# Attention over channels and a mixture of experts on one Trainium2 core: loads moved to GpSimd's queue, and the last block ended tile by tile over four pieces

## The chip, the core and the metric

The kernel runs on one core of one Trainium2 chip. The metric is the time of one execution in device microseconds (us). The core has five engines with an instruction queue each: TensorE (PE in the profile, its weight loads PEld), VectorE (DVE), ScalarE (ACT), GpSimd (POOL) and SyncE (SP). Each works through its own queue in order, and waits there for semaphores that others raise. SP does no arithmetic: it issues DMA transfers. GpSimd issues some too.

## The reference: what is computed

Channel attention over B = 4 batches of N = 5056 tokens with C = 256 channels, whose result goes into a mixture of eight experts, where each token goes to one expert alone:

```python
qn = q / (norm(q, axis=1) + 1e-06); kn = k / (norm(k, axis=1) + 1e-06)
a = softmax(kn.transpose(0, 2, 1) @ qn / tau, -1)         # per batch, 256 x 256
x = (v @ a).reshape(20224, 256)
logits = x @ w_gate + modality_bias[modality_id]          # 20224 x 8
e_idx = argmax(logits, 1); gate_w = softmax(logits, -1)[rows, e_idx]
out[mask] = gate_w[mask, None] * (relu(x[mask] @ w1[e]) @ w2[e])   # mask: e_idx == e, F = 1024
```

Norms run over the tokens of a batch, for each channel. All tensors are float32; `modality_id` is an int64 of 0 or 1.

## The kernel before

**Stages.** Batch 0's gram matrix (k transposed times q) is formed in ten steps of 512 tokens (the last is shorter). Then come its norms, its softmax and the product with v. From there on 40 token groups of 512 follow each other; group g is (batch, step) = divmod(g, 10). Each group is multiplied with its batch's attention matrix, its gates are computed, every token is given a place in its expert's part of a row buffer `xs` in DRAM, and its row is scattered there. From group 2 on, a block of 512 such rows of one expert is taken per group, so that 40 blocks (slots 0 to 39; the last two have three tiles of 128 rows, the others four) run through the expert's two matrix products, and the rows are scattered to `out`. The later batches' gram steps are laid between these. Blocks past slot 39 exist as conditional code, which this input does not reach.

**The gram, `kq_pieces`.** SP fetches q and k of a step (L305), TensorE multiplies (L355; in the order's rows `g`), ScalarE squares (L344, into `sq`), VectorE adds the squares into `acc` (L346). After step 9 VectorE folds `acc` (L402), TensorE sums over partitions (L405 and L407, `ns`), ScalarE and VectorE invert the roots (L412 to L426, `inv`, `rk`), ScalarE copies the gram out of PSUM (L434, `sc`), VectorE scales it (L438) and takes the maximum (L440), ScalarE exponentiates (L442), and VectorE normalises it to `ae` (L443 to L445). TensorE then turns it (L458, `atp`), forms the gates' weights from it (L478, `gw`), and multiplies with v (L624, `xp`); ScalarE copies the result out (L628, `x`).

**Small loads.** `load_small` fetches tau, the gates' weights and the modality bias at step 4, `load_mod` the modality numbers (`modraw`, five transfers) at step 5. `turn_mod` takes the lowest bit (L231, L237), turns it on TensorE (L240, `modtp`) and copies it to `m` on VectorE (L246, L249). GpSimd forms from it the bias of every token (`setup_bias`, L258 to L263). `pad_rows` (L180) writes 512 rows of zeros behind the experts' rows of `xs`.

**The block, `block_pieces`.** `load_x` (L779) reads the block's first row from the planner's number `pki`, and fetches the rows and their gate values (`gt`). The first two blocks (`slot < WHOLE_ROWS`) fetch whole rows (`xr`, L789), which TensorE turns (L858, `xtp`); later blocks fetch four pieces (L791), which VectorE turns (L554). The load waits until the scatters of all groups up to g have landed. `load_w` (L810) fetches half of an expert's weights at a time on SP (`w1r` L814, `w2r` L818); `split_w` splits them into a high and a low part (ScalarE L837, VectorE L844). Each of eight pieces j of 128 hidden columns has a first product on TensorE (`m1`, L882, `hp`: six matmuls), a relu on ScalarE (L885, `hh`), the low part on VectorE (L886, `hl`) and a second product (`m2`, L901, `y`: three matmuls per tile). `finish` scales a tile on ScalarE (L917, `yo`) and has GpSimd scatter it (L520).

**What sets the order.** The program writes pieces of several streams between each other. A scheduler then orders each engine's instructions and adds the semaphores. The transfers of one issuer take its eight semaphores in turn, so that an issue waits for the one eight before it.

## Time and profile before

| what | value |
|---|---|
| runs, median (lowest to highest) | 1176.22 us (1171.70 to 1181.63), 3 runs |
| profiled execution | 1182.62 us, its span 1181.0 us, mean granted TensorE clock 0.994 |
| instructions in the span | 22641 |
| busy PE / DVE / ACT / POOL | 1159.4 / 880.1 / 729.2 / 523.3 us |
| HBM read / written | 167.06 MB / 43.43 MB, 178 GB/s over the span |
| DMA: SP's queue / GpSimd's | 147.80 MB / 61.43 MB |

The profile is one execution; its times count from the start of its span. Its rows name line, engine, operation and operands by the program's names (buffer numbers left out). A timeline row gives start, duration, engine (SPq and POOLq are the sequencers), line, operation, operands and count, and in brackets the idle time before it with what ended that. A row of a view of waits gives the engine, its tile and line, whom it waited for, and total, times and longest. Matmuls overlap: 0.28 us of one and a step of 0.12 us to the next stand side by side.

### The profile page before, as it was taken

The numbers are of one execution on the slowest core, as the hardware profiler recorded it, in microseconds if no ns is written. First come the engines' busy times: TensorE is split into PE (matmuls) and PEld (weight loads), VectorE is DVE, ScalarE is ACT, GpSimd is POOL, SyncE is SP. The second block draws the span as 40 slices with busy tenths as digits, with TensorE's granted clock in tenths as the row PEclk, the third lists the DMA queues.
The fourth block names the chain that finished last, engine by engine and source line by source line (L and its number), as shares of the span: only waits on it lengthen the run. The fifth ranks groups of instructions, "written<-read, shape, count | busy, mean of one in ns | idle before, by whom it ended". The sixth has DMA issues, their size and how long they took to land.

```text
span 1181.0 us, 22641 instructions
## 1 busy us (share of the span) xinstructions
PE 1159.4 (98%) x7582; PEld 1056.4 (89%) x7582; DVE 880.1 (75%) x2154; ACT 729.2 (62%) x1449; POOL 523.3 (44%) x550
## 2 busy tenths in 40 slices
PE   9999999999999999999999999999999999999997
PEld 8888989899999999989999999998999999988997
DVE  6777988988788887797777778685677666675553
ACT  6565877866666666776666666565555555534553
POOL 1255534444444444435444545454444555564222
PEclk9999999999999999999999999999999999998999
DMA  8959778777776666676666575556566554553430
GB/s 323 302 200 265 214 234 208 177 179 189 189 188 187 192 177 199 166 205 167 186 197 195 172 206 147 146 152 159 143 174 171 149 166 145 148 141 116 126 109 30
DMA packets 173774, 210.77 MB, mean 178 GB/s; under 512 B 81448, under 2 KB 128040, under 8 KB 173648
## 3 DMA queue, kind: packets, MB, share of 16 engines
q1 hardware_dynamic: 149456, 147.80, 45.6%
q0 software_dynamic: 24192, 61.43, 17.7%
q8 instruction: 61, 1.00, 0.4%
q14 instruction: 65, 0.53, 0.2%
HBM read 167.06 MB, written 43.43 MB: 178 GB/s over the span
## 4 chain that ended last, share of the span: by engine, by line
PE 86%; DVE 5%; issue 5%; ACT 1%; DMA 1%; POOL 1%; another core or an unknown queue 1%; POOLq 0%; SPq 0%; DVEq 0%; ACTq 0%
PE y L901 34%; PE hp L882 34%; PE xp L624 9%; PE g L369 4%; PE g L355 3%; PE g L373 2%; DVE acc L346 2%; POOL out_dram L520 1%; DMA w2r<-in_moe_w_dram 0%; PE vtp L595 0%; DVE hl L886 0%; DMA k<-in_k_dram 0%; DVE w1l L844 0%; DVE w2l L844 0%
## 5 line engine op out<-in xcount | busy, mean ns | idle before, releaser
L901 PE MATMUL y<-w2h,hh 128*128 128x256 f32 x1264 | 355.1, 281 | 3.5 <-issue 2.7
L901 PE MATMUL y<-w2l,hh 128*128 128x256 f32 x1264 | 353.3, 280 | 2.4 <-issue 2.4
L901 PE MATMUL y<-w2h,hl 128*128 128x256 f32 x1264 | 351.4, 278 | 0.5 <-issue 0.4
L520 POOL DMA_INDIRECT xs<-x,pi x160 | 190.2, 1189 | 342.2 <-issue 163.2
L901 PEld LDWEIGHTS y<-w2h,hh 128*128 128x128 f32 x1264 | 238.3, 189 | 16.6 <-issue 3.0
L882 PE MATMUL hp<-xh,w1h 128*128 128x512 f32 (+1 forms) x640 | 252.7, 395 | 0.3 <-ACT xh L869 0.3
L882 PE MATMUL hp<-xl,w1h 128*128 128x512 f32 (+1 forms) x640 | 251.5, 393 | 0.5 <-DVE xl L870 0.5
L901 PEld LDWEIGHTS y<-w2l,hh 128*128 128x128 f32 x1264 | 238.9, 189 | 13.8 <-issue 2.8
L882 PE MATMUL hp<-xh,w1l 128*128 128x512 f32 (+1 forms) x640 | 249.7, 390 | 0.0
L886 DVE SCALAR_TENSOR_TENSOR hl<-hp,hh 128x512 fp32r<-128x512 f32 (+1 forms) x320 | 216.8, 677 | 41.6 <-ACT hh L885 33.4
L885 ACT ACTIVATE hh<-hp 128x512 fp32r<-128x512 f32 (+1 forms) x320 | 189.2, 591 | 83.5 <-PE hp L882 77.0
L901 PEld LDWEIGHTS y<-w2h,hl 128*128 128x128 f32 x1264 | 237.6, 188 | 1.3 <-issue 0.9
L520 POOL DMA_INDIRECT out_dram<-yo,gt x158 | 174.0, 1101 | 109.4 <-ACT yo L917 63.5
L844 DVE TENSOR_TENSOR w1l<-w1r,w1h 128x512 fp32r<-128x512 f32 x160 | 110.4, 690 | 121.8 <-ACT w1h L837 99.0
L791 POOL DMA_DIRECT2D xr<-xs x152 | 102.7, 685 | 159.6 <-DMA xs<-x,pi 73.2
L837 ACT CAST w1h<-w1r 128x512 fp32r<-128x512 f32 x160 | 98.7, 617 | 120.2 <-PE hp L882 106.6
L844 DVE TENSOR_TENSOR w2l<-w2r,w2h 128x512 fp32r<-128x512 f32 x160 | 109.0, 682 | 62.1 <-ACT w2h L837 60.4
L882 PEld LDWEIGHTS hp<-xh,w1l 128*128 128x128 f32 x640 | 120.6, 188 | 26.0
L882 PEld LDWEIGHTS hp<-xh,w1h 128*128 128x128 f32 x640 | 120.5, 188 | 14.7 <-ACT xh L869 0.6
L882 PEld LDWEIGHTS hp<-xl,w1h 128*128 128x128 f32 x640 | 120.5, 188 | 14.2 <-DVE xl L870 1.0
L837 ACT CAST w2h<-w2r 128x512 fp32r<-128x512 f32 x160 | 100.3, 627 | 45.5 <-PE y L901 34.1
L628 ACT COPY x<-xp 128x264 f32<-128x264 f32 x160 | 61.0, 382 | 96.7 <-PE xp L624 67.8
(162 smaller groups left out, 1824.7 us busy)
## 6 DMA issues: line engine op xcount, KB each, us to landing
w1r<-in_moe_w_dram SPq DMA_DIRECT2D x80, 512.0 KB
w2r<-in_moe_w_dram SPq DMA_DIRECT2D x80, 512.0 KB
q<-in_q_dram SPq DMA_DIRECT2D x36, 512.0 KB
k<-in_k_dram SPq DMA_DIRECT2D x36, 512.0 KB
xr<-xs POOLq DMA_DIRECT2D x144, 128.0 KB
v<-in_v_dram SPq DMA_DIRECT2D x112, 128.0 KB
v<-in_v_dram SPq DMA_DIRECT2D x8, 512.0 KB
xs<-x,pi POOLq DMA_INDIRECT x160
```

The lines of the kernel that those rows point to most:

```text
L355: nc.tensor.matmul(g[:, 0:C], st["k"][:pp, 2 * h + t, m::CH], st["q"][:pp, 2 * h + t, :], start=first, stop=last, skip_group_check=True,)
L369: nc.tensor.matmul(g, ks[:pp, t, m * P : (m + 1) * P], qs[:pp, t, :], start=first, stop=False, skip_group_check=True,)
L520: ins = nc.gpsimd.indirect_dma_start(out=dst, out_offset=bass.IndirectOffsetOnAxis(ap=idx, axis=0), in_=rows, in_offset=None, bounds_check ...
L624: nc.tensor.matmul(xp[:, 0:DE], a[:, h, t * P : (t + 1) * P], w[:, h, :], start=i == 0, stop=i == len(seq) - 1,)
L628: nc.scalar.copy(st["x"][:, t, :], xp[:, 0:DE])
L791: eng.dma_start(xr[j * Q : (j + 1) * Q, 0 : rows // Q, :], src[:, j * CQ : (j + 1) * CQ].rearrange("(i t) c -> t i c", t=Q),)
L837: ins = nc.scalar.copy(hi, src).ins
L844: nc.vector.tensor_tensor(lo, src, hi.bitcast(F32), ALU.subtract)
L882: nc.tensor.matmul(hp[:, 0:rows], w[:, h, fs], x[:, h, 0:rows], start=i == 0, stop=i == len(seq) - 1)
L885: nc.scalar.activation(hh[:, 0:rows], hp[:, 0:rows], AF.Relu)
L886: low = nc.vector.scalar_tensor_tensor(hl[:, 0:rows], hp[:, 0:rows], 0.0, hh[:, 0:rows].bitcast(F32), ALU.max, ALU.subtract)
L901: ins = nc.tensor.matmul(y, a[:, tsl], w[:, j % 2, :], start=(j == 0 and i == 0 and t % 2 == 0), stop=(j == NJ - 1 and i == 2), skip_group ...
```

## The change

It has four parts.

1. The small loads, the modality loads and the write of zero rows are issued from GpSimd's queue instead of SP's, and the zero rows are written at step 1 of batch 0 instead of before the loop over groups.
2. `load_x` of slots 0 and 1 is issued by GpSimd too, as for all others.
3. In slot 39 the second products of j = 4 are done by tile, together with those of j = 5, 6 and 7.
4. The `hh` and `hl` of that block's last piece take other buffers (tag `sq` of pool `p2`).

```diff
--- before.py
+++ after.py
@@ -179,7 +179,7 @@
 
     def pad_rows():
 
-        ins = nc.sync.dma_start(
+        ins = nc.gpsimd.dma_start(
             xs[E * CAP : E * CAP + BLK, :].rearrange("(p t) c -> p t c", t=BLK // P),
             pad[0].unsqueeze(1).to_broadcast([P, BLK // P, XW]),
         )
@@ -192,12 +192,12 @@
 
     def load_small():
         itau = small["itau"] = const.tile([P, 1], F32, name="itau")
-        nc.sync.dma_start(itau, tau.partition_broadcast(P))
+        nc.gpsimd.dma_start(itau, tau.partition_broadcast(P))
         nc.vector.reciprocal(itau, itau)
         wg_sb = small["wg"] = const.tile([P, CH, E], F32, name="wg_sb")
-        nc.sync.dma_start(wg_sb, wg.rearrange("(h p) e -> p h e", p=P))
+        nc.gpsimd.dma_start(wg_sb, wg.rearrange("(h p) e -> p h e", p=P))
         mb_sb = small["mb"] = const.tile([P, 2, E], F32, name="mb_sb")
-        nc.sync.dma_start(
+        nc.gpsimd.dma_start(
             mb_sb.rearrange("p m e -> p (m e)"), mb.rearrange("m e -> (m e)").partition_broadcast(P)
         )
 
@@ -215,11 +215,11 @@
         nc.vector.memset(raw[full // 32 * 32 : R, 2 * PL * TT : 2 * STEP], 0)
         m32 = mod.bitcast(I32).rearrange("(b n) -> b n", b=B)
         for b in range(B):
-            nc.sync.dma_start(
+            nc.gpsimd.dma_start(
                 raw[b * (NS - 1) : (b + 1) * (NS - 1), 0 : 2 * STEP],
                 m32[b, 0 : 2 * (NS - 1) * STEP].rearrange("(s w) -> s w", w=2 * STEP),
             )
-        nc.sync.dma_start(raw[full:R, 0 : 2 * PL * TT], m32[:, 2 * (NS - 1) * STEP : 2 * N])
+        nc.gpsimd.dma_start(raw[full:R, 0 : 2 * PL * TT], m32[:, 2 * (NS - 1) * STEP : 2 * N])
         turn["raw"] = raw
 
     def turn_mod():
@@ -776,7 +776,7 @@
         turns = [0, 2, 1, 3][:tt] if tt > 2 else list(range(tt))
 
         def load_x():
-            eng = nc.sync if slot < WHOLE_ROWS else nc.gpsimd
+            eng = nc.gpsimd
             r = eng.value_load(pki[0:1, 0:1], min_val=0, max_val=E * CAP)
             if slot < WHOLE_ROWS:
                 xr = p2.tile([P, TT, D], F32R, tag="xr", name=f"xr_{slot}")
@@ -880,8 +880,9 @@
             ]
             for i, (w, x, h) in enumerate(seq):
                 nc.tensor.matmul(hp[:, 0:rows], w[:, h, fs], x[:, h, 0:rows], start=i == 0, stop=i == len(seq) - 1)
-            hh = p3.tile([P, BLK], F32R, tag="hh", name=f"hh_{slot}_{j}")
-            hl = p3.tile([P, BLK], F32R, tag="hl", name=f"hl_{slot}_{j}")
+            end = slot == NB_MIN - 1 and j == NJ - 1
+            hh = (p2 if end else p3).tile([P, BLK], F32R, tag="sq" if end else "hh", name=f"hh_{slot}_{j}")
+            hl = (p2 if end else p3).tile([P, BLK], F32R, tag="sq" if end else "hl", name=f"hl_{slot}_{j}")
             nc.scalar.activation(hh[:, 0:rows], hp[:, 0:rows], AF.Relu)
             low = nc.vector.scalar_tensor_tensor(
                 hl[:, 0:rows], hp[:, 0:rows], 0.0, hh[:, 0:rows].bitcast(F32), ALU.max, ALU.subtract
@@ -903,7 +904,7 @@
                         start=(j == 0 and i == 0 and t % 2 == 0), stop=(j == NJ - 1 and i == 2),
                         skip_group_check=True,
                     ).ins
-                    if slot == NB_MIN - 1 and j >= NJ - 3:
+                    if slot == NB_MIN - 1 and j >= NJ - 4:
 
                         at = turns.index(t)
                         if at > 0:
@@ -938,14 +939,14 @@
             body.append(lambda j=j: m1(j))
             if (j + 1) % 2 == 0 and (j + 1) // 2 + 1 < NJ // 2:
                 body.append(lambda j=j: split_w((j + 1) // 2 + 1))
-            if j > 1 and (slot != NB_MIN - 1 or j < NJ - 1):
+            if j > 1 and (slot != NB_MIN - 1 or j < NJ - 2):
 
                 body.append(lambda j=j: m2(j - 2))
         if slot == NB_MIN - 1:
 
             last = []
             for t in turns:
-                last += [lambda j=j, t=t: m2(j, range(t, t + 1)) for j in range(NJ - 3, NJ)]
+                last += [lambda j=j, t=t: m2(j, range(t, t + 1)) for j in range(NJ - 4, NJ)]
                 last.append(lambda t=t: finish(t))
         else:
             last = [lambda: m2(NJ - 2), lambda: m2(NJ - 1)] + [lambda t=t: finish(t) for t in range(tt)]
@@ -964,6 +965,8 @@
         run(kq_pieces(0, s))
         if s == 0:
             make_pad("pad0")
+        if s == 1:
+            pad_rows()
         if s == 4:
             load_small()
         if s == 5:
@@ -1035,7 +1038,6 @@
             run(kq_pieces(1, s))
         else:
             run(kq_pieces(1, s, lambda: routed[0] + turned[1], squares[s]))
-    pad_rows()
     for g in range(G):
         b, s = divmod(g, NS)
         streams = []
```

The scheduler moves other instructions with these. TensorE, in batch 0's gram (`g`: gram; `modtp`: the turned modality bits; q and k carry the step's number). Before, the turn stands ahead of step 6:

```order
L355 MATMUL g_0_172<-q_5_300,k_5_302 128x256
L355 MATMUL g_0_173<-q_5_300,k_5_302 128x256
L240 MATMUL modtp<-ident,modlow 128x40 x4
L355 MATMUL g_0_172<-q_6_331,k_6_333 128x256
L355 MATMUL g_0_173<-q_6_331,k_6_333 128x256
```

In the changed kernel it stands ahead of step 9:

```order
L355 MATMUL g_0_172<-q_8_380,k_8_382 128x256
L355 MATMUL g_0_173<-q_8_380,k_8_382 128x256
L240 MATMUL modtp<-ident,modlow 128x40 x4
L355 MATMUL g_0_172<-q_9_417,k_9_419 128x256
L355 MATMUL g_0_173<-q_9_417,k_9_419 128x256
```

The copies that follow it on VectorE, on whose result GpSimd's bias work waits, move in the same way. VectorE before (`acc`: the sums of squares, `sq` with step, half and tensor; `m`: the modality bits):

```order
L346 TENSOR_TENSOR acc_174<-acc_174,sq_5_0_k 128x2x256
L346 TENSOR_TENSOR acc_174<-acc_174,sq_5_1_k 128x2x256
L231 TENSOR_SCALAR modlow<-modraw 40x512
L237 CAST modlow<-modlow 40x512
L246 COPY m_132<-modtp 128x36 x4
L249 COPY m_132<-modtp 128x4x4
L346 TENSOR_TENSOR acc_174<-acc_174,sq_6_0_q 128x2x256
```

and of the change:

```order
L346 TENSOR_TENSOR acc_174<-acc_174,sq_9_1_k 112x2x256
L402 TENSOR_TENSOR acc_174<-acc_174 128x512
L246 COPY m_132<-modtp 128x36 x4
L249 COPY m_132<-modtp 128x4x4
L346 TENSOR_TENSOR acc_537<-acc_537,sq_0_1_q 128x2x256
L346 TENSOR_TENSOR acc_537<-acc_537,sq_0_1_k 128x2x256
L415 TENSOR_SCALAR inv_446<-inv_446 128x258
L422 RECIPROCAL inv_446<-inv_446 128x129
```

So the copies come behind the fold of the squares, and ahead of the softmax chain (`acc_537` are batch 1's sums). On TensorE one gram matmul row of batch 1 moves from before the first turn of the softmax (L458) to behind it.

GpSimd's queue, after its setup (the scatters of a group's four tiles are one row; `x_675`, `x_792`, `x_897` and `x_1026` belong to groups 2, 3, 4 and 5; `xr_1662` are the rows of block 2). Before:

```order
L520 DMA xs<-x_675,pi_862 168448x258 x4
L520 DMA xs<-x_792,pi_991 168448x258 x4
L520 DMA xs<-x_897,pi_1096 168448x258 x4
L780 TENSOR_LOAD pki_1123
L780 ISA x2
L520 DMA xs<-x_1026,pi_1233 168448x258 x4
```

and of the change (`xr_1153`, `gt_1154`: rows and gates of block 0; `xr_1313`, `gt_1314`: of block 1):

```order
L520 DMA xs<-x_675,pi_862 168448x258 x4
L780 TENSOR_LOAD pki_889
L780 ISA x2
L789 ISA
L789 DMA xr_1153<-xs 128x4x256
L797 ISA
L797 DMA gt_1154<-xs 128x4x2
L520 DMA xs<-x_792,pi_991 168448x258 x4
L780 TENSOR_LOAD pki_1018
L780 ISA x2
L789 ISA
L789 DMA xr_1313<-xs 128x4x256
```

The two blocks' loads stand between the groups' scatters, group 4's scatters come behind block 1's load, and block 2's first piece comes ahead of group 5's scatters, its other three behind them. On SP the second half of block 0's weights now follows the first half directly, where the two loads of block 0's rows and gates stood between.

The end of TensorE's queue, in slot 39 (`hp_6`, `hp_7`: first products of j = 6 and 7; `hh_4` to `hh_7`: the pieces j of the second products). Before, from the last matmul of hp_6 on:

```order
L882 MATMUL hp_6_16805<-xh_16579,w1l_3_16748 128x384
L901 MATMUL y_39_16725<-w2h_2_16710,hh_4_16771 128x256
L901 MATMUL y_39_16725<-w2l_2_16711,hh_4_16771 128x256
L901 MATMUL y_39_16725<-w2h_2_16710,hl_4_16772 128x256
```

of which there are three sets, one for each tile, and then hp_7 and the rest by tile. In the changed kernel:

```order
L882 MATMUL hp_6_16805<-xh_16579,w1l_3_16748 128x384
L882 MATMUL hp_7_16816<-xh_16579,w1h_3_16747 128x384
L882 MATMUL hp_7_16816<-xl_16580,w1h_3_16747 128x384
L882 MATMUL hp_7_16816<-xh_16579,w1l_3_16748 128x384
```

hp_7 (six matmuls) follows hp_6 directly, and then each tile has twelve second products, j = 4 to 7, instead of nine.

## The prediction, made before the changed kernel ran

> **What bounds the kernel now.** The page's busy times name TensorE. So I read the windows by stage first, then TensorE's waits, and last the timeline at the few places where TensorE stands still. The windows (length, busy time by engine with counts, granted TensorE clock, DMA share, GB/s):
>
> ```profile
> 0.00:100.00 100.00, 91.76 (x535) 83.01 (x536) 74.30 (x237) 61.98 (x135) 35.48 (x45) 0.98 0.80 273
> 100.00:1050.00 950.00, 947.80 (x6285) 862.79 (x6284) 741.62 (x1819) 609.08 (x1207) 442.25 (x455) 1.00 0.66 179
> 1050.00:1075.00 25.00, 19.96 (x96) 16.83 (x95) 10.14 (x19) 6.37 (x12) 11.41 (x13) 0.80 0.38 100
> 1075.00:1165.00 90.00, 90.00 (x603) 84.43 (x602) 51.84 (x77) 48.36 (x93) 31.23 (x35) 1.00 0.38 111
> 1165.00:1181.00 16.00, 9.85 (x72) 9.37 (x70) 2.23 (x4) 3.37 (x7) 2.92 (x3) 0.96 0.09 30
> ```
>
> TensorE is full in the second and fourth rows (947.80 of 950, 90.00 of 90). No matmul is added or taken away, so an edit there is worth nothing unless it makes TensorE wait. What can be won lies in the first row (8.2 us idle, some of it start-up), the third (5.0 us) and the last (6.2 us). The waits in the first and last row are small enough to be taken one by one.
>
> **The first softmax.** VectorE adds squares (L346) until L402, and TensorE stands from the end of batch 0's gram to the norms:
>
> ```profile
> 27.31 14.09 PE L355 MATMUL g<-q,k 128*128 128x256 f32 x64
> 43.19 0.67 PE L405 MATMUL ns<-acc,ones 128*128 128x256 f32 x2 [1.79 <-DVE acc L402]
> ```
>
> VectorE is late because GpSimd forms the modality bias beside it. Pairs of adds take 2.03 to 2.50 us while GpSimd works (from 28.10 on) and 1.49 after:
>
> ```profile
> 27.92 2.03 DVE L346 TENSOR_TENSOR acc<-acc,sq_q 128x512 f32<-128x512 f32 x2
> 28.10 0.58 POOL L258 TENSOR_SCALAR m<-m 128x40 f32<-128x40 f32 x1 [17.98 <-DVE m L249]
> 29.87 2.37 DVE L346 TENSOR_TENSOR acc<-acc,sq_k 128x512 f32<-128x512 f32 x2
> 32.16 2.14 DVE L346 TENSOR_TENSOR acc<-acc,sq_q 128x512 f32<-128x512 f32 x2
> 34.22 2.50 DVE L346 TENSOR_TENSOR acc<-acc,sq_k 128x512 f32<-128x512 f32 x2
> 36.64 1.49 DVE L346 TENSOR_TENSOR acc<-acc,sq_q 128x512 f32<-128x512 f32 x2
> 42.36 0.69 DVE L402 TENSOR_TENSOR acc<-acc 128x512 f32<-128x512 f32 x1
> ```
>
> Four pairs cost 9.04 us where 4 x 1.49 = 5.96 would do: 3.08 us too many, a factor of 1.52. The change moves the copies of the modality bits (L246, L249) behind L402, so these adds run alone. L402 then ends near 43.05 - 3.08 = 39.97, before the gram's end at 41.40, and the 1.79 us go.
>
> The bias work then lies beside the softmax chain, on which TensorE's next step depends:
>
> ```profile
> 44.68 0.30 DVE L415 TENSOR_SCALAR inv<-inv 128x258 f32<-128x258 f32 x1 [1.03 <-ACT inv L412]
> 45.01 0.96 DVE L422 RECIPROCAL inv<-inv 128x129 f32<-128x129 f32 x1
> 45.89 0.91 DVE L424 RECIPROCAL inv<-inv 128x129 f32<-128x129 f32 x1
> 46.87 0.88 DVE L438 SCALAR_TENSOR_TENSOR sc<-sc,rk,inv 128x256 f32<-128x256 f32 x2
> 47.67 0.74 DVE L440 TENSOR_REDUCE smx<-sc 128x1 f32<-128x256 f32 x2
> 49.31 0.34 DVE L445 TENSOR_SCALAR ae<-sc,ssm 128x256 f32<-128x256 f32 x1
> 49.87 0.38 PE L458 MATMUL atp<-ident,ae 128*128 128x128 f32 x2
> ```
>
> The result is there at 49.65 and TensorE takes it at 49.87: 0.22 us to spare. One gram matmul row of batch 1 (two matmuls of 0.22 us, from the 14.09 us of 64) is moved behind this step, so 0.23 us of waiting appears. Of the chain, only L438 reads two full tensors, as the slowed adds do; slowed by 1.52 it costs 0.88 x 0.52 = 0.46. If all five operations from L415 to L440 (0.30 + 0.96 + 0.91 + 0.88 + 0.74 = 3.79 us) were slowed it would be 1.97. No row shows a reduction or a reciprocal beside a GpSimd operation, so these are the ends; I take 0.46, by the row it resembles. The front is then -1.79 + 0.23 + 0.46 = **-1.1**, between -1.8 (chain untouched) and +0.5 (chain wholly slowed).
>
> The Trainium skill ("SBUF — State Buffer", section "SBUF: two separate sides") says that VectorE and GpSimd share one pair of ports as an exclusive lock, which a VectorE operation with two SBUF inputs takes against a GpSimd operation that reads SBUF. The rows of the adds agree (1.49 against 2.03 to 2.50); by that rule the reciprocals and reductions go free, and the front would be the -1.1 above.
>
> **Loads moved to GpSimd's queue.** The small loads, the modality loads and the zero rows are now issued early, beside q and k. The zero rows are 512 x 1032 bytes, 0.53 MB; at the window's 273 GB/s they delay the stream by up to 1.9 us. Batch 0's gram waits once for a load, 0.92 us at the start, and then never:
>
> ```profile
> 6.05 20.97 PE L355 MATMUL g<-q,k 128*128 128x256 f32 x96 [0.92 <-DMA k<-in_k_dram]
> 6.00:14.00 8.00, 7.95 (x37) 7.28 (x38) 7.13 (x20) 7.42 (x14) 0.27 (x2) 1.00 1.03 420
> ```
>
> A step of 16 matmuls takes 3.5 us and its 1 MB takes 2.5 us at 420 GB/s, so the lead grows by 1 us a step. Bounds 0 to +1.9; I take **0**, since the cover is TensorE's own gram.
>
> **Rows of the first two blocks on GpSimd.** They wait for the scatters of the groups before them, on SP now:
>
> ```profile
> 89.42 2.91 POOL L520 DMA_INDIRECT xs<-x,pi  x1 [0.30 <-DVE sm L687]
> 89.56 0.02 SPq L789 DMA_DIRECT2D xr<-xs  x1
> 92.82 0.74 PE L858 MATMUL xtp<-identr,xr 128*128 128x128 f32 x4 [0.89 <-DMA xr<-xs]
> L791 POOL DMA_DIRECT2D xr<-xs x152: 618/682/802, 107.3 to 1113.7; - x152
> ```
>
> TensorE waits for block 0's rows already (0.89 us), so whatever the load loses is lost. GpSimd spends 0.68 us on such a load where SP's row shows 0.02: +0.66, which I round to **+0.7**. Bounds: 0, and +2.9, the longest GpSimd issue here, if the issue is held up as that scatter was.
>
> By the Trainium skill ("DMA: Bandwidth & Descriptors", section "SWDGE vs HWDGE vs iDMA") SP's path sets up faster than GpSimd's, and its table gives 0.6 against 1 us to the first byte. That speaks against this edit; by those figures the term would be an estimated +0.4 and the whole sum 0.3 lower, near 1173.8.
>
> Behind the waiting load on GpSimd stand g3's four scatters, of which the row at 89.42 is one; before, two of them went ahead of it. They would start near 91 (89.56, 0.68 for the rows and about as much for the gates), end near 96 at 1.27 each (the spacing of the last block's scatters, below), and if they land as the row load does, 3.3 us from issue to use (89.56 to 92.82), block 1's load is issued near 99.5 and is there near 103. TensorE turns it at 109.59 without a wait, so over 6 us remain. Block 2's four pieces move from 107.3 to some 10 us later; VectorE turns them first at 144.6:
>
> ```profile
> 109.59 0.67 PE L858 MATMUL xtp<-identr,xr 128*128 128x128 f32 x4
> L554 DVE STREAM_TRANSPOSE xt<-xr x38: 969/1234/1239, 144.6 to 1151.7; 128x1024 f32<-128x1024 f32 x36, 128x768 f32<-128x768 f32 x2
> ```
>
> That leaves over 20 us. In exchange SP is free of the row loads, and block 0's second half of weights (issued 90.46) comes sooner. ScalarE, in order, waited for it, and TensorE's 0.7 us on hh follow from that:
>
> ```profile
> PE y L901 <- ACT hh L885: 0.7, 1, 0.7
> 97.45 1.14 ACT L837 CAST w2h<-w2r 128x512 fp32r<-128x512 f32 x2 [1.20 <-DMA w2r<-in_moe_w_dram]
> ```
>
> I take **-0.7**, bounds -0.7 and 0.
>
> **The end.** In the last block (three tiles) j = 4's nine matmuls now stand behind hp_7:
>
> ```profile
> 1171.12 0.28 PE L901 MATMUL y<-w2h,hh 128*128 128x256 f32 x1
> 1172.88 0.48 ACT L917 ACTIVATE yo<-y,gt 128x256 f32<-128x256 f32 x1 [1.07 <-PE y L901]
> 1173.62 0.28 PE L901 MATMUL y<-w2h,hl 128*128 128x256 f32 x1
> 1173.63 0.97 POOL L520 DMA_INDIRECT out_dram<-yo,gt  x1 [9.70 <-ACT yo L917]
> 1174.67 0.27 PE L901 MATMUL y<-w2h,hl 128*128 128x256 f32 x1
> 1174.98 0.47 ACT L917 ACTIVATE yo<-y,gt 128x256 f32<-128x256 f32 x1 [0.56 <-PE y L901]
> 1176.18 0.98 POOL L520 DMA_INDIRECT out_dram<-yo,gt  x1 [0.30 <-issue]
> ```
>
> From the second tile's last matmul (1173.62) to the third's (1174.67) are nine steps, so one takes 0.117 us. The first behind hp_7 starts at 1171.12, and the last, 26 steps on, could start at 1171.12 + 26 x 0.117 = 1174.16: TensorE stands 0.5 us, while the first tile waits for hh and hl of j = 7. In the change hp_7 ends 9 x 0.117 = 1.05 earlier, and the first tile uses the last hl after eleven matmuls instead of eight, so this stall goes. TensorE's last matmul then starts at 1174.16, ScalarE's yo follows 0.31 later as now (1174.67 to 1174.98), and the scatter 0.75 behind that (1172.88 to 1173.63): 1175.22 instead of 1176.18. The first tile's output comes 1.05 earlier and holds up nothing, since the scatters are (1176.18 - 1173.63) / 2 = 1.27 apart and 1172.58 + 2.54 = 1175.12. That is **-1.0**, between -0.5 (only TensorE's stall) and -1.1 (the scatters follow the first).
>
> **Sum**: -1.1 + 0 + 0.7 - 0.7 - 1.0 = **-2.1 us**. The profiled execution took 1182.62 us (span 1181.0 and 1.6 around it) and would take 1180.5. It is 6.4 above the median of the runs, 1176.22. The third window's row (5.0 us idle, clock 0.80) is about that size and is not touched. The median becomes **1174.1**.
>
> **Rivals.**
>
> *Only the end gains.* The bias work slows the chain by 1.56 instead of 0.46 (0.23 + 1.56 = 1.79), and the loads cancel. For it: the chain has 0.22 us to spare and the bias work, which slowed adds from 27.92 to 36.64, is long enough to cover all of it. Against: only L438 resembles the slowed adds. Time: 1176.22 - 1.0 = 1175.2.
>
> *Slower: block 0's rows are held on GpSimd.* Place: xtp, L858. If the load loses the full 2.9 us, TensorE stands 3.8 us. After the wait of 1.89 us for x the clock fell to half, as it did not after the 1.79 before the norms:
>
> ```profile
> 72.74 0.39 PE L624 MATMUL xp<-ah,vh 128*128 128x264 f32 x1 [1.89 <-ACT x L628]
> 75.00:76.00 1.00, 1.00 (x6) 1.00 (x6) 0.97 (x5) 0.48 (x3) 0.00 (x0) 0.50 0.45 123
> ```
>
> The slices from 74 to 77 show 0.50 like this one, and the next 0.85: 3 x 0.5 + 0.15, about 1.7 us more, and so 2.9 + 1.7 - 1.1 - 1.0 = +2.5, or 1178.7 (the weights' gain is void, since TensorE waits for the rows). It decides once the load is over 2.1 us late. Against: from block 2 on GpSimd loads so all the time, at 0.62 to 0.80.
>
> *The stall at 71 us goes.* Different queue order may let ScalarE deliver x in time: 1.89 + 1.7 = 3.6 less, 1170.5. Nothing names a DMA as its cause, hence little chance.
>
> That the change doesn't do what it says is excluded: the order shows each move.
>
> **How the numbers follow.** Forecast 0.5, only the end 0.22, slower 0.14, stall gone 0.14. The terms' bounds together reach from -1.8 - 0.7 - 1.1 = -3.6 to +0.5 + 1.9 + 2.9 - 0.5 = +4.8, that is 1172.6 to 1181.0; the runs of before themselves scatter by 5 us, and the rival of the stall reaches 1170.5 before that, so I give 1166.5 to 1181. One per cent, 11.8 us, is about what a measurement can tell from no change: under 1164.5 or over 1188.0. No case reaches either; 0.08 and 0.04 are left for stalls like that of the third window coming or going, 0.88 is within.
>
> **What would show it.** L246 behind L402; pairs of adds at 1.49; no wait before the norms, a wait of about 0.7 before atp; L438 slower beside L260; xtp waiting about 1.6; hp_7 ahead of all of j = 4's second matmuls and no stall of TensorE behind it. Wrong if xtp waits over 3 us, if reciprocals stretch beside GpSimd, if gram matmuls wait for k past 6 us, or if TensorE waits in the middle stages.

## The result, and the profile after

The changed kernel takes 1190.81 us (median of seven runs, 1182.39 to 1195.23) against 1176.22 for the kernel before (seven runs, 1171.70 to 1182.65). The ratio is 1.009, with a 95% interval of 1.0063 to 1.0117: slower by about one per cent, where 1174.1 was predicted. (The quotient of the two medians is 1.012, just above that interval; the ratios here and below are those of the measurements, not quotients of medians.)

The two profiled executions hide this: 1182.62 us before, 1182.39 after. The stage windows show why (length, busy time by engine with counts, granted TensorE clock, DMA share, GB/s). After:

```profile
0.00:100.00 100.00, 89.07 (x511) 80.55 (x512) 69.52 (x223) 59.07 (x129) 33.27 (x52) 0.98 0.85 282
100.00:1050.00 950.00, 944.67 (x6241) 857.89 (x6240) 736.75 (x1775) 605.15 (x1200) 440.54 (x453) 1.00 0.65 177
1050.00:1075.00 25.00, 25.00 (x162) 22.47 (x162) 19.75 (x78) 12.23 (x22) 18.91 (x20) 1.00 0.55 146
1075.00:1165.00 90.00, 90.00 (x603) 84.39 (x602) 52.14 (x78) 48.33 (x92) 32.09 (x37) 1.00 0.39 114
1165.00:1181.00 16.00, 9.77 (x73) 9.47 (x71) 2.23 (x4) 3.39 (x7) 2.94 (x3) 0.90 0.09 30
```

Read the counts beside the busy times: at half clock TensorE is busy and does half as much. In the first 100 us there are 24 matmuls fewer (511 against 535), in the next 950 us 44 fewer (6241 against 6285). The third row has 66 more (162 against 96): the execution of before had a stall there, this one has none. The starts of one and the same matmul make this a ladder. Before (duration least/median/most in ns, first and last start):

```profile
L882 PE MATMUL hp<-xh,w1h x1: 393/393/393, 299.6 to 299.6; 128*128 128x512 f32 x1
L882 PE MATMUL hp<-xh,w1h x1: 393/393/393, 1038.4 to 1038.4; 128*128 128x512 f32 x1
L882 PE MATMUL hp<-xh,w1h x1: 393/393/393, 1093.1 to 1093.1; 128*128 128x512 f32 x1
```

After:

```profile
L882 PE MATMUL hp<-xh,w1h x1: 393/393/393, 309.6 to 309.6; 128*128 128x512 f32 x1
L882 PE MATMUL hp<-xh,w1h x1: 393/393/393, 1048.4 to 1048.4; 128*128 128x512 f32 x1
L882 PE MATMUL hp<-xh,w1h x1: 393/393/393, 1093.3 to 1093.3; 128*128 128x512 f32 x1
```

The changed kernel is 10.0 us behind at 300 us and still 10.0 at 1038; then the execution of before loses 9.8 us in its stall (ScalarE waits 8.1 us at a cast of w2h, and the clock falls to half). The two totals alone would make the change free. What the change costs lies before 300 us.

TensorE's waits in the changed kernel (engine, tile, line, whom it waited for: total, times, longest) name two places:

```profile
PE xtp L858 <- DMA xr<-xs: 5.4, 1, 5.4
PE y L902 <- ACT yo L918: 1.5, 1, 1.5
PE hp L882 <- DVE hl L887: 1.4, 2, 0.8
```

**Block 0's rows** (xtp) wait 5.4 us instead of 0.9. The timeline of GpSimd and TensorE there (start, duration; in brackets the idle time before):

```profile
83.63 0.98 POOL L520 DMA_INDIRECT xs<-x,pi  x1 [0.30 <-issue]
90.75 0.83 POOL L789 DMA_DIRECT2D xr<-xs  x1 [6.13 <-DMA xs<-x,pi]
96.94 0.78 PE L858 MATMUL xtp<-identr,xr 128*128 128x128 f32 x4 [5.44 <-DMA xr<-xs]
```

The window with the low clock:

```profile
95.88:102.71 6.83, 5.77 (x19) 4.76 (x20) 3.49 (x14) 2.94 (x7) 1.43 (x2) 0.50 0.96 343
```

The last scatter of group 2 is issued at 84.61 (83.63 + 0.98) and has landed 6.1 us later, when GpSimd issues the rows; from there to xtp, the first matmuls that use the rows, 6.2 us pass. Before, it was 3.7 and 3.3: the scatter's issue at 84.90 took 0.98, the rows went out at 89.56, xtp began at 92.82. From 95.88 to 102.71 the granted clock is 0.50, where before it stayed at 1.00, and that costs up to 2.9 us more (half of the 5.77 us in which TensorE worked there).

**Batch 1's last step**, q_9, is the second place. ScalarE waits for its q and, being in order, keeps block 2's outputs (yo) waiting behind it:

```profile
192.74 0.62 ACT L320 CAST qs<-q 112x512 fp32r<-112x512 f32 x1 [5.29 <-DMA q<-in_q_dram]
198.46 1.55 ACT L918 ACTIVATE yo<-y,gt 128x256 f32<-128x256 f32 x4
```

and the window from 180 to 300 us:

```profile
180.00:300.00 120.00, 116.26 (x762) 104.30 (x761) 98.97 (x230) 83.21 (x166) 51.91 (x53) 1.00 0.71 183
```

Before, two of the yo stood ahead of that cast, and it needed no wait:

```profile
190.36 0.84 ACT L917 ACTIVATE yo<-y,gt 128x256 f32<-128x256 f32 x2 [0.48 <-PE xp L624]
191.34 0.64 ACT L320 CAST qs<-q 112x512 fp32r<-112x512 f32 x1
```

and its window:

```profile
180.00:300.00 120.00, 119.49 (x790) 108.34 (x789) 103.04 (x247) 86.28 (x174) 52.02 (x52) 1.00 0.75 189
```

28 matmuls of that stretch are missing after (762 against 790), some 4 us at the 0.15 us that one takes there on average (119.49 / 790).

**Whose transfers are in the way** is seen in the DMA view between the end of the last scatter's issue and the rows' issue (q1 is SP's queue, q0 GpSimd's: packets, MB, share of the 16 engines' time). Before, 85.88 to 89.56:

```profile
q0 software_dynamic: 189, 0.52, 38.0%
q1 hardware_dynamic: 179, 0.17, 13.1%
```

After, 84.61 to 90.75:

```profile
q1 hardware_dynamic: 1970, 1.65, 94.1%
q0 software_dynamic: 144, 0.40, 16.1%
```

While the scatters land, SP's queue moves ten times as much as before. Those bytes are the second half of block 0's weights (SP issues it at 81.56, at 90.46 before) and pieces of v (from 86.59, at 91.78 before). On SP both had stood behind the rows.

The front and the end came out as the change meant them. VectorE and TensorE in the first softmax:

```profile
31.14 1.48 DVE L346 TENSOR_TENSOR acc<-acc,sq_k 128x512 f32<-128x512 f32 x2
39.65 0.69 DVE L402 TENSOR_TENSOR acc<-acc 128x512 f32<-128x512 f32 x1
43.33 0.60 PE L405 MATMUL ns<-acc,ones 128*128 128x256 f32 x2
47.04 0.88 DVE L438 SCALAR_TENSOR_TENSOR sc<-sc,rk,inv 128x256 f32<-128x256 f32 x2
49.81 0.41 PE L458 MATMUL atp<-ident,ae 128*128 128x128 f32 x2 [0.15 <-DVE ssm L443]
```

The adds run at 1.48 a pair, L402 is over 2.7 us earlier, and the norms need no wait. They are no earlier all the same, since the gram itself ended late in this execution (below). The end, from the first matmul of hp_6 to the last scatter:

```profile
1168.13 0.34 PE L882 MATMUL hp<-xh,w1h 128*128 128x384 f32 x1
1175.56 0.98 POOL L520 DMA_INDIRECT out_dram<-yo,gt  x1 [0.41 <-issue]
```

That is 7.43 us, against 8.23 before, where hp_6 began at 1167.95 and the last scatter at 1176.18.

### The profile page after: what moved, and what is told of

Read it like the earlier page. It is cut to its first block, busy times and chain, and to the rows that moved or that the text cites. A ratio compares the mean times of both kernels' runs of the same rounds, so it can differ in the third digit from the quotient of the medians.

```text
span 1180.7 us, 22635 instructions
## 1 busy us (share of the span) xinstructions
PE 1158.5 (98%) x7582; PEld 1054.8 (89%) x7582; DVE 880.4 (75%) x2154; ACT 728.2 (62%) x1449; POOL 527.8 (45%) x563
## 4 chain that ended last, share of the span: by engine, by line
PE 87%; issue 5%; DVE 3%; DMA 2%; ACT 1%; POOL 1%; POOLq 0%; SPq 0%; ACTq 0%; DVEq 0%
PE y L902 34%; PE hp L882 34%; PE xp L624 9%; PE g L369 4%; PE g L355 4%; PE g L373 2%; POOL out_dram L520 1%; DMA q<-in_q_dram 1%; DVE acc L346 1%; DMA xs<-x,pi 1%; DMA xr<-xs 1%; DMA k<-in_k_dram 0%; DVE hl L887 0%; PE vtp L595 0%; PE atp L458 0%
## 5 line engine op out<-in xcount | busy, mean ns | idle before, releaser
L882 PE MATMUL hp<-xh,w1h 128*128 128x512 f32 (+1 forms) x640 | 253.1, 396 | 1.4 <-DVE hl L887 1.4
L882 PE MATMUL hp<-xl,w1h 128*128 128x512 f32 (+1 forms) x640 | 251.6, 393 | 0.0
L882 PE MATMUL hp<-xh,w1l 128*128 128x512 f32 (+1 forms) x640 | 249.6, 390 | 0.0
L882 PEld LDWEIGHTS hp<-xh,w1l 128*128 128x128 f32 x640 | 120.5, 188 | 26.0 <-issue 0.2
L882 PEld LDWEIGHTS hp<-xh,w1h 128*128 128x128 f32 x640 | 120.6, 189 | 16.4 <-DVE hl L887 1.8
L882 PEld LDWEIGHTS hp<-xl,w1h 128*128 128x128 f32 x640 | 120.4, 188 | 13.5 <-DVE xl L870 0.2
```

The costliest lines, as they stand in the source:

```text
L882: nc.tensor.matmul(hp[:, 0:rows], w[:, h, fs], x[:, h, 0:rows], start=i == 0, stop=i == len(seq) - 1)
```

## The experiments

**Theory.** SP's wait for block 0's rows was a gate. As long as SP stood there, it issued neither the second half of block 0's weights, nor the pieces of v, nor block 1's weights. With the rows on GpSimd nothing holds SP: its transfers take the DMA engines first from the scatters for which the rows wait, and then from the rows. **Rivals:** GpSimd's own path is slow (its issue, or its queue); the small loads or the early zero rows disturb the front's traffic; block 1's load, not block 0's, does it; most of the loss is the second place (q_9), which the scheduler made. The experiments ran on other occasions, in three rounds on three chips: the first four on chip 0, the next four on chip 10, the last four on chip 6. The kernel before takes 1167.98, 1167.72 and 1167.73 us there, against 1176.22 in the measurement above, so each run is compared by its ratio to before on its own chip (95% interval).

### One part undone, one part alone

The changed kernel with the two blocks' rows back on SP:

```diff
         def load_x():
-            eng = nc.gpsimd
+            eng = nc.sync if slot < WHOLE_ROWS else nc.gpsimd
```

> The changed kernel with one part undone: the rows and gates of blocks 0 and 1 are loaded from SP's queue again; small loads, zero rows and the last block's order stay as changed. Theory (the row load lost its place at the head of SP's queue, so that weights and v pieces go out ahead of it and take the DMA engines, and the scheduler's order in the middle of batch 1 changed with it): all of the loss is in this part, so about 10 us come back; 0.1 to 0.3 per cent faster than before or no difference, xtp waiting about 1 us, no q wait of TensorE's suppliers at 190 us. Rival (the small loads and zero rows on GpSimd crowd the early transfers): still about 1 per cent slower than before.

Measured: 1166.52 against 1167.98, ratio 0.9992 (0.9982 to 1.0003). xtp waits 1.8 us, and the stretch from 180 to 300 us is full again (120.00 busy of 120). Without the rows' move the loss is gone.

The kernel before with the rows on GpSimd, and nothing else:

```diff
         def load_x():
-            eng = nc.sync if slot < WHOLE_ROWS else nc.gpsimd
+            eng = nc.gpsimd
```

> The kernel before with one part of the change alone: rows and gates of blocks 0 and 1 loaded from GpSimd's queue. Theory: this part alone costs 0.8 to 1.0 per cent (about 10 us); xtp waits over 4 us for xr, the clock falls to half for one or two stretches of 3.4 us behind it, and a second loss of some 4 us comes between 180 and 300 us. Rival (small loads): no difference from before. If the rows' load costs only GpSimd's longer issue: 0.1 per cent slower, xtp waiting about 1.6 us.

Measured: 1176.39 against 1167.98, ratio 1.0077 (1.006 to 1.0095). Its last scatter of group 2, the rows, xtp, and the window around block 0:

```profile
80.81 0.97 POOL L520 DMA_INDIRECT xs<-x,pi  x1 [0.30 <-issue]
88.02 0.85 POOL L789 DMA_DIRECT2D xr<-xs  x1 [6.23 <-issue]
95.76 0.77 PE L858 MATMUL xtp<-identr,xr 128*128 128x128 f32 x4 [7.93 <-DMA xr<-xs]
```

and

```profile
84.00:104.00 20.00, 12.07 (x66) 10.25 (x65) 9.50 (x43) 7.56 (x19) 8.77 (x10) 0.74 0.90 257
```

Both losses come from the rows alone: xtp waits 7.9 us, the clock is at half from 90.98 to 101.22 (three times 3.41 us, where one or two were expected), and ScalarE waits 4.2 us for q at 190 us (TensorE busy 118.26 of the 120 us from 180 to 300). The second loss is smaller than the 4 us expected, some 2 to 3 us (below).

Only part 1, the small loads and the zero rows:

```diff
-        nc.sync.dma_start(itau, tau.partition_broadcast(P))
+        nc.gpsimd.dma_start(itau, tau.partition_broadcast(P))
...
+        if s == 1:
+            pad_rows()
```

> The kernel before with one part of the change alone: small loads, modality loads and zero rows issued from GpSimd. Theory: within 0.2 per cent of before; the norms wait no longer (1.79 us before), the adds of squares take 1.49 us a pair, and the softmax chain keeps its times. Rival (this part carries the loss): 0.5 to 1 per cent slower.

Measured: 1166.45, ratio 0.9987 (0.9976 to 0.9999). No wait before the norms, 0.7 us before atp, xtp waits 1.7. The rival of the small loads falls: they gain, if anything.

Only parts 3 and 4, the end:

```diff
-                    if slot == NB_MIN - 1 and j >= NJ - 3:
+                    if slot == NB_MIN - 1 and j >= NJ - 4:
...
-                last += [lambda j=j, t=t: m2(j, range(t, t + 1)) for j in range(NJ - 3, NJ)]
+                last += [lambda j=j, t=t: m2(j, range(t, t + 1)) for j in range(NJ - 4, NJ)]
```

> The kernel before with one part of the change alone: the last block's second products of j = 4 done by tile too. Both theories: about 1.0 us faster, which is under 0.1 per cent and not to be seen in the time; in the profile TensorE does not stand behind hp_7, and the last scatter starts 4.1 us after hp_7's first following matmul would have (1176.18 - 1171.12 = 5.06 before) less one.

Measured: 1168.09, ratio 1.0004 (0.9992 to 1.0016): a gain of 0.8 us is 0.0007 and lies inside the interval. Since this kernel has the order of before up to its last block, its profile, on chip 0, serves as the reference for the ones that follow:

```profile
81.70 0.97 POOL L520 DMA_INDIRECT xs<-x,pi  x1 [0.31 <-issue]
...
85.90 0.39 SPq L789 DMA_DIRECT2D xr<-xs  x1
89.91 0.73 PE L858 MATMUL xtp<-identr,xr 128*128 128x128 f32 x4 [1.20 <-DMA xr<-xs]
```

and

```profile
84.00:104.00 20.00, 18.12 (x114) 16.00 (x113) 16.95 (x66) 11.11 (x25) 13.12 (x12) 1.00 0.87 240
```

From the end of the last scatter's issue (82.67) to the rows' issue 3.2 us pass, from there to xtp 4.0. TensorE does 114 matmuls in the window where the rows on GpSimd leave 66.

### What in the rows' move costs

The rows alone, with the second half of block 0's weights held on SP until the scatters have landed:

```diff
+            first = nc.sync.dma_start(
                 a,
...
+            if slot == 0 and hf == 1:
+                for before in range(g + 1):
+                    after(first.ins, written[before])
```

> Rows of blocks 0 and 1 alone on GpSimd, as in the second run, and the second half of block 0's weights on SP made to wait for the same scatters as the row load, so that SP again stands still until the rows may go; the order of instructions on all engines is that of the second run. Theory (transfers that SP no longer holds back take the DMA engines from the scatters and the rows): xtp's wait falls from 7.9 us to 2 to 4 us, and the time from 0.8 to 0.3 to 0.5 per cent over before, the rest being the order in the middle of batch 1. Rival (GpSimd's own path makes the row load slow): xtp still waits about 8 us.

Measured: 1174.81 against 1167.72, ratio 1.0058 (1.0041 to 1.0075), xtp waits 5.9. The number was missed, and the rows show how:

```profile
87.10 0.56 SPq L814 DMA_DIRECT2D w1r<-in_moe_w_dram  x1
...
88.06 0.85 POOL L789 DMA_DIRECT2D xr<-xs  x1 [4.17 <-issue]
95.79 0.78 PE L861 MATMUL xtp<-identr,xr 128*128 128x128 f32 x4 [5.85 <-DMA xr<-xs]
```

In this and the next runs "the scatters land in" means the time from the end of the last scatter's issue to the issue of the rows. Here it is 4.2 us, but the weights are released by the same event and go out 1 us ahead of the rows, which then take 7.7 us. The first delay is cured, the second stays.

The kernel before, rows on SP, but placed behind the second half of the weights:

```diff
-            prep, ahead = prep[:1] + ahead + prep[1:], []
+            prep, ahead = prep + ahead, []
```

> The kernel before, all on SP, with the rows of block 0 loaded behind the second half of its weights instead of ahead of it; ScalarE's, VectorE's and TensorE's order is that of before. Theory: the 1 MB of weights goes out some 8 us earlier and delays the scatters or the rows, so xtp waits 1 to 3 us more than before's 0.9 to 1.2; 0.1 to 0.3 per cent slower. Rival (GpSimd's path): no difference from before.

Measured: 1170.30, ratio 1.0021 (1.0012 to 1.0031), xtp waits 3.4. GpSimd's path isn't used for the rows at all, and still the scatters land late, in 5.1 us; the rows themselves then take 4.3, since SP still holds block 1's weights back:

```profile
88.95 0.38 SPq L789 DMA_DIRECT2D xr<-xs  x1
93.29 0.78 PE L858 MATMUL xtp<-identr,xr 128*128 128x128 f32 x4 [3.43 <-DMA xr<-xs]
```

There is no second loss (120.00 busy of 120 from 180 to 300 us).

Only block 0's rows on GpSimd, block 1's on SP:

```diff
-            eng = nc.sync if slot < WHOLE_ROWS else nc.gpsimd
+            eng = nc.sync if slot == 1 else nc.gpsimd
```

> The kernel before with the rows of block 0 alone loaded from GpSimd's queue; block 1's stay on SP, where they still hold back block 1's weights. Theory: block 0's rows still lose, because its weights' second half and the v pieces go ahead, but block 1's 2 MB of weights are held until block 1's rows may go: xtp waits 3 to 6 us instead of 7.9, 0.4 to 0.6 per cent slower than before. Rival (GpSimd's path): as in the second run, 0.77 per cent.

Measured: 1171.28, ratio 1.0033 (1.002 to 1.0046), below the 0.4 to 0.6 per cent expected; xtp waits 4.6, within. The scatters land in 6.2 us, as with both blocks moved; but SP now stands at block 1's rows until 97.06, and with it block 1's weights, and the rows take 4.45 us instead of 7.7.

Only block 1's rows on GpSimd:

```diff
-            eng = nc.sync if slot < WHOLE_ROWS else nc.gpsimd
+            eng = nc.sync if slot == 0 else nc.gpsimd
```

> The kernel before with the rows of block 1 alone loaded from GpSimd's queue. Theory: block 0's rows keep their place, so xtp waits 1 to 2 us; what is left is the changed order in the middle of batch 1, 0 to 0.3 per cent slower than before. Rival (GpSimd's path): block 1's xtp waits too, by several us.

Measured: 1168.70, ratio 1.0002 (0.9991 to 1.0013), xtp waits 1.0. Block 1's load alone costs nothing that the totals show (in its trace TensorE waits 1.9 us for hh instead of 0.7, with 3.41 us at half clock behind that). The two do not add up (1.0033 and 1.0002 against 1.0077 for both): in each of them SP still stands at the other block's rows, and holds something back there, as the rows' times show (4.45 us in the first, 7.7 with both).

Both on GpSimd, and the second half of block 0's weights held until the rows have landed:

```diff
+            st["rows"] = [moved[0].ins]
...
+            if slot == 0 and hf == 1:
+                after(first.ins, st["rows"])
```

> Rows of blocks 0 and 1 on GpSimd, and the second half of block 0's weights on SP held until block 0's rows have landed; the order of the engines differs a little from the second run's, and one piece of v goes out ahead of the hold. Theory (what slows the rows is the traffic that SP used to hold back): GpSimd's load takes 4 to 5 us from its issue to xtp instead of 7.7, and xtp waits 2 to 3.5 us instead of 7.9; the weights come late instead, so the whole is 0.2 to 0.6 per cent slower than before. Rival (GpSimd's own path): 7 us or more from issue to xtp as in the second run.

Measured: 1170.58 against 1167.73, ratio 1.002 (1.0011 to 1.003), xtp waits 2.2:

```profile
87.46 0.85 POOL L789 DMA_DIRECT2D xr<-xs  x1 [3.95 <-issue]
91.75 0.74 PE L861 MATMUL xtp<-identr,xr 128*128 128x128 f32 x4 [2.19 <-DMA xr<-xs]
```

From the end of the last scatter's issue (82.53 + 0.97) to the rows' issue it is 3.95 us, and from 180 to 300 us TensorE is busy throughout. With the gate put back by hand, GpSimd's load costs little. Of what is left (0.2%) the profile shows three pieces: xtp waits 1.0 us longer than in the reference, 3.41 us at half clock follow, and TensorE waits 1.2 us for hh (0.7 in the reference), as the weights start only at 91.73, after the rows. Which of them the total goes to isn't separated.

The six kernels side by side (the first and the fifth ran on chip 0, the last on chip 6, the others on chip 10): time from the end of the last scatter's issue to the rows' issue, MB that SP's queue moves in it, time from the rows' issue to xtp, MB of other transfers that SP's queue moves in that (rows taken off where they are SP's own, 0.52 MB).

| kernel | landing, us | SP's MB | rows, us | SP's other MB | ratio |
|---|---|---|---|---|---|
| end only (rows on SP, order of before) | 3.2 | 0.15 | 4.0 | 0.2 | 1.0004 |
| rows behind the weights, on SP | 5.1 | 1.25 | 4.3 | 0.1 | 1.0021 |
| block 0's rows on GpSimd | 6.2 | 1.59 | 4.45 | 0.19 | 1.0033 |
| both on GpSimd, weights held for the scatters | 4.2 | 0.15 | 7.7 | 1.40 | 1.0058 |
| both on GpSimd | 6.2 | 1.63 | 7.7 | 1.53 | 1.0077 |
| both on GpSimd, weights held for the rows | 3.95 | 0.28 | 4.3 | 0 | 1.002 |

Each time is long exactly where SP's queue moves over 1 MB in it, with the rows on either queue; where it moves little, GpSimd's load is issued 0.7 to 1.0 us later and takes at most 0.5 longer to arrive. The changed kernel's own profile lies between for the rows: 6.2 us beside 0.97 MB (landing 6.1 beside 1.65). Landing includes what passes between the last packet and the issue: in the DMA view GpSimd's queue moves nothing from 86.4 to 88.0 us with both on GpSimd, and nothing from 85.7 to 87.4 with the weights held for the rows. So the scatters' packets are through some 4.6 and 2.2 us after the last issue (81.78 and 83.50), and in both kernels 1.6 to 1.8 us more pass.

The groups that this rests on are of the DMA view, from the rows' issue to xtp. With both on GpSimd and the weights held for the scatters (88.06 to 95.79):

```profile
q1 hardware_dynamic: 2206, 1.40, 71.0%
q0 software_dynamic: 206, 0.62, 28.9%
```

and with the weights held for the rows (87.46 to 91.75), SP's queue has no row at all:

```profile
q0 software_dynamic: 224, 0.66, 54.8%
```

GpSimd's 0.62 and 0.66 MB (rows and parts of scatters) take 7.7 us beside 1.40 MB of SP's and 4.3 us alone. Its packets themselves are hardly slowed: they keep the 16 engines for 28.9% of 7.73 us, 2.23 us, in the first and for 54.8% of 4.29 us, 2.35 us, in the second. In the first the two queues' shares add up to 100%: the engines are taken throughout, so what is left is that GpSimd's packets wait for their turn. The Trainium skill ("DMA: Bandwidth & Descriptors", section "Queues, rings and completion order") says that a DMA engine takes its queue rows in turn, a packet at a time, and that what one sequencer issues is taken in ring order. The rows agree: on SP's queue the later weights stood behind the rows; on GpSimd's the rows share the engines with them.

### The second place

The rows alone, with ScalarE's work on q_9 ordered behind block 2's outputs:

```diff
         def act(ins):
+            if b == 1 and s == 9:
+                order(ins.ins, ended)
...
+            if slot == 2:
+                ended.append(scaled.ins)
```

> The second run's kernel (rows of blocks 0 and 1 alone on GpSimd), with ScalarE's work on q and k of batch 1's last gram step tied behind block 2's outputs, where it stood before. Theory (in the changed order ScalarE reaches that q 4 to 5 us before it has landed, and TensorE then waits for outputs and hl): the loss between 180 and 260 us goes, 2.3 us of the second run's 9; the first loss at block 0's rows stays, 0.55 to 0.65 per cent over before. Rival (the second loss is the late rows' own echo, further down the pipeline): as slow as the second run, 0.77.

Measured: 1175.72 against 1167.73, ratio 1.0067 (1.0054 to 1.0079). The cast of q_9 has no wait (it starts at 197.43, behind the yo at 195.75), and TensorE none for yo; the stretch is nearly full (119.10 of 120). The total is just over the 0.55 to 0.65 per cent expected, and its interval overlaps that of the rows alone, so the totals don't decide between theory and rival. In this execution xtp waits 9.5 us.

The changed kernel once more, on chip 6, and beside it the changed kernel with the same ordering as above:

> The changed kernel once more, on the chip of the other runs. Theory: the sum of its parts as measured apart, 0.65 to 0.85 per cent slower than before (rows 0.77, small loads -0.13, end 0.0). If it is 0.9 or more, the parts do not add up and something in their combination is missed.

> The changed kernel with ScalarE's work on q and k of batch 1's last gram step tied behind block 2's outputs. Theory: 2 to 5 us less than the changed kernel (its trace showed 4.7 us lost between 180 and 300 us), 0.3 to 0.6 per cent over before. Rival (echo of the late rows): no difference from the changed kernel.

Measured: 1175.92, ratio 1.0068 (1.0052 to 1.0083), and 1174.14, ratio 1.006 (1.0047 to 1.0073). The changed kernel again (its cast of q_9, at 192.26, waits 5.1 us):

```profile
89.25 0.83 POOL L789 DMA_DIRECT2D xr<-xs  x1 [7.33 <-DMA xs<-x,pi]
97.18 0.77 PE L858 MATMUL xtp<-identr,xr 128*128 128x128 f32 x4 [9.08 <-DMA xr<-xs]
```

and

```profile
180.00:300.00 120.00, 117.85 (x777) 106.54 (x776) 101.13 (x240) 84.95 (x170) 51.76 (x53) 1.00 0.71 183
```

and with q_9 ordered behind (the cast starts at 192.44 without a wait):

```profile
180.00:300.00 120.00, 119.64 (x794) 108.65 (x793) 103.15 (x242) 85.88 (x172) 52.59 (x55) 1.00 0.74 190
```

The ordering takes the wait away and gives most of the missing matmuls back (794 against 777). The starts of the same first products (L882) size it: from the 145th to the 193rd TensorE takes 28.2 us with the end alone, 30.4 with the rows alone and 31.1 in the changed kernel, and with q_9 ordered behind 28.6 and 28.7. So ScalarE's wait costs 2 to 3 us there, and that isn't an echo of the late rows: with the ordering it goes, although xtp waited 9.5 us before. Up to the 289th the times are 86.7, 89.2, 89.9, 88.1 and 87.4: part of the loss comes back later in a way that the runs don't explain. In the totals it is the smaller part and not clear of the noise: 1.8 us between the two medians, under the 2 to 5 expected, with overlapping intervals. The bulk is block 0's rows. The parts add up, too: 1.0077 x 0.9987 x 1.0004 = 1.0068, which is what the whole change takes on chip 6. (Each interval reaches some 0.0012 to 0.0018 either way, so that the last digit agrees by chance.)

## Why the prediction was wrong

**The step that failed** is the pair of terms on the rows of the first two blocks: +0.7 us for the load and, "in exchange", -0.7 for weights that come sooner, together 0. At that place the runs show a loss of 6.7 us. The first was priced as a dearer issue (0.68 against 0.02 us), with the longest issue of GpSimd, 2.9 us, as its upper bound. The 0.02 was a poor yardstick: in the profiles of the other chips where block 0's rows go by SP the same row shows 0.38 or 0.39. The size was about right all the same for what it priced: with the weights held for the rows, GpSimd's path costs 0.7 us more to the issue and 0.3 more to arrival. The figures of the Trainium skill ("DMA: Bandwidth & Descriptors", section "Specifications": 1 against 0.6 us to the first byte) are of that size too, and say nothing of what followed. What it left out is the other half of "SP is free": everything that SP had kept back is issued at once. The second term had the wrong sign. The weights' second half did come sooner, by 8.9 us, and TensorE's 0.7 us for hh went, as forecast. For that, the scatters landed 2.4 us later and the rows took 2.9 us longer (6.1 and 6.2 us against 3.7 and 3.3), and the half clock took up to 2.9 more. Matmuls on either side give the sum: a product of rp (L667) ahead of the place starts at 76.74 against 78.02, 1.3 us early, and block 0's first y product at 104.56 against 99.14, 5.4 us late. The place cost 6.7 us, where the forecast had 0.

**The rival "block 0's rows are held on GpSimd"** named the place (xtp), the sign and the half clock, and the test "wrong if xtp waits over 3 us" is met by 5.4 (and by 7.9 and 9.1 in the rows alone and in the changed kernel's second profile). But its mechanism, an issue held up as the scatter at 89.42 was, isn't what happened: the issue takes 0.83 us. And its price, 2.9 + 1.7, was too small because it knew only one of the two delays. The argument against it, that GpSimd loads so from block 2 on at 0.62 to 0.80 us, spoke of the issue and not of the transfer. The row that would have warned was quoted: 420 GB/s with a DMA share of 1.03 shows what unhindered loads of SP do to the engines.

**A term was missing altogether**: the second place. The forecast followed the engines' order at the places that the edit touches, and not what the scheduler makes of it 100 us later on ScalarE. The reordering of ScalarE comes from the rows' move: with the rows alone the cast of q_9 stands ahead of all four yo (190.01 against 195.96), while with the small loads alone or the end alone it stands behind them (187.66 against 185.97; 187.75 against 186.06). "Wrong if TensorE waits in the middle stages" was met as well, by 1.5 us for yo and 1.4 for hl.

**The front** was right in its mechanism: no slow adds (1.48 a pair), L402 at 39.65 (39.97 predicted), the bias work beside the softmax chain. L438 was not slowed (0.88 us, as before), but that says nothing of the argument behind the 0.46: GpSimd's last bias operation started at 46.95 and took 0.23 us, and L438 began at 47.04. The bias work was too short to reach it, 6.3 us (40.93 to 47.18) instead of the 8.7 (28.10 to 36.80) that it took beside the adds. In the run of the small loads alone it met another operation of the chain: L415 took 0.94 us instead of 0.30 and atp waited 0.7, a loss of about the size forecast, at a place where none was. The bounds given for the front don't follow from its terms either: -1.79 + 0.23 is -1.56 and not -1.8, and with 1.97 more it is +0.41 and not +0.5; that changes nothing in the outcome. Measured alone the front gives 1.5 us (0.9987; the interval reaches from 0.1 to 2.8), against 1.1 predicted; with it the rival "only the end gains", in which the chain eats this gain, falls as far as that interval goes. **The small loads** cost nothing that the runs show: batch 0's gram waits once for k, 0.7 us (once, 0.9, before). **The end** gave 0.8 us in the trace, against 1.0; the stall behind hp_7 is gone. In the totals it can't be seen (1.0004, 0.9992 to 1.0016).

**Block 1's rows and block 2's pieces** cost nothing, as predicted: xtp waits only once. **The stall at 71 us** did go in the profiled execution (clock 1.00 from 66 to 80 us, 0.88 before), as the third rival had it, but not by the change: on the other chips no profile has it, with the old queues or the new (with the end alone, which keeps before's queues, TensorE is busy 13.76 of these 14 us). The rival named something that comes and goes with the execution; the loss behind it is larger.

**What stays open.** In the measurement of the result the median is 14.6 us up, on chip 6 it is 8.2. The first profiled execution of the changed kernel has no stall near 1060 us and took 1182.39; its six other runs took 1189 to 1195, with a mean clock of 0.990 to 0.994 instead of 0.996. A stall as in the execution of before, 9.8 us, would fit both, but none of these six has a profile, and no profile of the other three chips has that stall. What causes it, and whether the change makes it more frequent, wasn't settled.

## What to carry to other kernels

An in-order queue that waits is also a gate for everything behind it. Before a waiting transfer is moved to another queue, list what stands behind it, in bytes, and ask which transfer on the critical path will share the DMA engines with that: here 0.7 us of dearer issue was counted, and the 1.65 MB that SP moved while the scatters landed was not. Keep the gate by a dependence if the move is wanted, or leave the load where its wait is useful; the small loads' move alone (0.9987, 0.9976 to 0.9999) is the only version tried that beats the kernel before, and barely. And compare two profiles by the starts of the same matmul along the span, not by their totals: one stall in one of them hid the whole loss.

## What the runs showed of the hardware

- **Half clock after short waits, in steps of 3.41 us.** With the small loads alone a wait of 1.71 us at xtp (its first matmul starts at 89.01) is followed by 3.41 us at half clock:

```profile
90.25:93.66 3.41, 3.41 (x12) 2.76 (x11) 3.01 (x13) 1.55 (x5) 2.50 (x4) 0.50 1.09 295
```

  The changed kernel with the rows back on SP waited 1.76 us there and kept clock 1.00. Nor does one and the same wait always do it: the wait of 1.8 us before the norms was followed by 3.41 us at half clock in two profiles (the rows alone with q_9 ordered back, from 45.00; the weights held for the rows, from 45.15) and not in the profile before or that of the end alone. So the length of a wait doesn't decide it; what does wasn't settled. Waits of 5.4 and 7.9 us gave two and three such stretches (6.83 and 10.2 us). The Trainium skill ("TensorE: Matmul & The Clock Gate", section "What's actually happening") describes a free-running window of 3.4 us, with the clock down after at least one idle window; the lengths agree, but half clock followed 1.71 us of idle time here, half such a window.
- **The start is worth 2 us either way.** From 6 to 8 us TensorE does 5 gram matmuls in some executions and 9 to 11 in others. After, and below it the rows alone, as one of each:

```profile
6.00:8.00 2.00, 2.00 (x5) 1.62 (x6) 1.31 (x3) 1.85 (x4) 0.00 (x0) 1.00 0.45 180
```

```profile
6.00:8.00 2.00, 1.97 (x9) 1.85 (x10) 1.24 (x2) 1.21 (x3) 0.00 (x0) 1.00 1.07 348
```

  The granted clock reads 1.00 in both, so that only the counts tell. (The trace's clock records begin at 10.55 us in the one and at 5.64 in the other; the column shows 1.00 for the time ahead of its first record.) It happens with the old small loads as well (5 also with the rows placed behind the weights), and not always with the new ones (9 with the small loads alone). In all, four of the five profiles with the new small loads have the slow start and two of the nine with the old: too few to say whether the change makes it likelier. It is why the front's gain isn't seen in the changed kernel's own profile.
- **A slowed add, and unslowed reciprocals.** Beside GpSimd's bias work (40.93 to 47.18 us after the change) single adds took 1.26 and 1.13 us instead of 0.69, and L415 took 0.94 instead of 0.30 in the run of the small loads alone; the reciprocals (0.96, 0.91) kept their times. The reduction (L440, at 47.84) came after that work, so no run shows one beside it.
